# A parallel attention and feed-forward kernel: a unit's first attention product three steps ahead of the rest, and seven small moves of splits, a relu, additions and a norm

## The chip, the cores and the metric

The kernel runs on one core of a Trainium2 chip. The core has five engines that work through their own instruction lists in order and wait for each other through semaphores: PE (TensorE, matmuls; PEld is its weight load), DVE (VectorE), ACT (ScalarE), POOL (GpSimd) and SP (SyncE, which here only issues DMAs; POOL issues some, too). The metric is the device time of one execution in microseconds.

## What is computed

```python
# x (1, 2048, 576); wqkv (576, 1728); wo (576, 576); w1 (576, 4608); w2 (4608, 576), fp32
def attention(xn):                  # 32 heads of 18
    q, k, v = split(xn @ wqkv)
    idx = pos[:, None] - 2 * arange(8)[None, :]     # 8 taps, two rows apart
    logits = where(idx >= 0, einsum("bhsd,bhswd->bhsw", q, k[idx]) * 18 ** -0.5, -1e9)
    return einsum("bhsw,bhswd->bhsd", softmax(logits), v[idx]) @ wo

xn = (x - mean(x)) / sqrt(var(x) + 1e-5)
return x + attention(xn) + relu(xn @ w1) @ w2
```

## The kernel before

**Phases and precision.** The taps are two rows apart, so even and odd rows never meet in the attention. The kernel works in two phases `ph`, the even rows and the odd rows, 1024 rows each in four token blocks `tb` of 256. Every fp32 factor is split into a high part and a remainder (`hi`, `lo`), and a product is three matmuls. `two` (L171) makes such a split: ACT copies the high part (L172), DVE subtracts to get the low part (L176), or POOL does where `pooled` is set (L174). The relu is split in the same manner (`relu_parts`, L765): ACT L769 writes the high part, DVE L773 the low part. `c_parts` calls it for one block of the hidden layer.

**Feed-forward.** The first 6 of a phase's 36 blocks of 128 hidden columns are done in 24 plain slots of one block and one token block each. The other 30 are done in pairs by a Strassen scheme: 30 groups `g` of eight steps (`group`, and `step` inside it). Two groups share one pair of W1 blocks (the even group is the first), and each group does two of the four token blocks. `sw_prep` splits the combined W1 matrices of a pair (A11, A12, A22, S1 to S4 and a remainder "rem"), `sw_mix` forms them on POOL (L924), `w2_split` splits W2. Products collect in PSUM banks called a, q, r and f, which come from the rings `ph` (a, q) and `pm` (r, f) of two buffers each. `seed` (L992, ACT) copies one bank into a new one, `keep` (L996, ACT) puts a bank aside as m5 or u3 (named m and u in the profile), `plus` (L1001, DVE) adds a bank to it. The second layer collects in `po`, and `evict` (L722, ACT; then a POOL DMA at L728 that accumulates in memory) takes it out. `prologue` is group 0 with the last slots woven in; `tail_end`, `last_group`, `seam` and `epilogue` finish a phase. In a step, `rows` issues the matmuls of the first layer, `after` their followers, `fire` the events of a table, and `o_half` the second layer.

**Attention.** The heads are done in four units `u` of 8 heads. Unit 0 is projected in the slots, units 1 to 3 in groups 5, 11 and 17 and the one after each (`QKV_G`), with the weights split by `wq_split`. From two groups later, 7, 13 and 19, the unit's attention is put on a background list `bg` of DVE operations: per tap window i a product (`qk_mul`, L575) and a sum (`qk_sum`, L578), then the softmax, then products and additions with V (L610, L617) and a transposition (L622). The first window, i = 7, reads only the unit's own rows; later ones read rows that `halos` fetches by DMA. `run_bg(margin)` takes operations off this list as long as the planner's clock of DVE does not pass that of PE by more than the margin; a small or negative margin takes fewer. The list's place in the program is thus the order on DVE.

**Output projection.** The attention's result goes through memory (`od`) and comes back transposed. `ot_plan` lists its work: `wo_rest` loads three pieces of WO (DMA, L267; event "wl"), `wo_split` splits each (ACT L172 `wq<-att` 128x576) a given time on the planner's clock after "wl", `ot_in` loads the result, `ot_split` (L683 to L685) splits it. `ot_one` issues at most one item at each place where it is asked, in every step.

**Start.** In the first slots of phase 0 the x rows are loaded in eight blocks, normalised (`stats`, then `norm`: L340 on DVE, or L337 and L338 on ACT with `act`), and transposed on PE (`make_xt`: L359 and L366 on ACT, L362 and L369 on DVE take the parts). `o_out` adds x to the first output blocks on DVE (L888).

## Time and profile before

| | us |
|---|---|
| median of 3 runs | 1127.75 |
| lowest and highest | 1126.84, 1128.8 |
| profiled execution, its own time | 1129.04 |
| span of its profile, first to last instruction | 1127.3 |
| mean granted TensorE clock | 0.998 |
| PE busy | 1108.6 |
| DVE busy | 850.8 |
| ACT busy | 571.0 |
| POOL busy | 367.9 |

A row of a timeline reads: start in us from the start of the span, duration, engine, line of the kernel, operation, result <- inputs with their shapes, a count, and in square brackets how long the engine stood idle before it and on what that ended. Where a tile is named `ar`, it is the arena of split weights and hidden blocks; `st` holds the staged weights, `ev` what is evicted, `att` the attention's arena, `pr` its products, and `xT`, `xS` the transposed rows and their Strassen sums. A tile with two buffers or more has one name for all.

### The profile page before, as it was taken

Reading aid. Unit: us, or ns where it says so; the run is one execution under the profiler, and the core shown is the slowest. Engines: PE = TensorE matmul, PEld = TensorE weight load, DVE = VectorE, ACT = ScalarE, POOL = GpSimd, SP = SyncE. Lnnn points to the kernel's source line nnn. Section 1 sums busy time; section 2 is a strip of 40 time slices with the busy share of each in tenths; the row PEclk is TensorE's granted clock in tenths of the full one; section 3 lists DMA queues with packets and bytes.
Section 4 is the critical chain, followed back from the end, with each engine's and each line's share of the span. In section 5 each row is a group of like instructions: output and inputs, shape, how many; then the busy total and the mean of one; then the engine's idle time right before and its main releaser. Section 6 shows DMA issues by size and latency. Waiting matters only on the chain.

```text
span 1127.3 us, 37950 instructions
## 1 busy us (share of the span) xinstructions
PE 1108.6 (98%) x16410; PEld 1093.4 (97%) x16410; DVE 850.8 (75%) x1249; ACT 571.0 (51%) x1348; POOL 367.9 (33%) x382
## 2 busy tenths in 40 slices
PE   8999999999999999999999999999999999999998
PEld 8999999999999999999999999999999999999998
DVE  7676898798898898984327339978888988989651
ACT  4433563564465356566434346535645644655550
POOL 2314342333333234433322225323413423344321
PEclk9999999999999999999999999999999999999999
DMA  7369895795696497889957258759848956878995
GB/s 235 125 170 221 180 186 90 152 201 105 123 218 128 87 208 144 161 163 267 264 82 156 44 124 169 131 93 216 167 80 175 189 103 152 164 153 154 197 178 135
DMA packets 136598, 177.26 MB, mean 157 GB/s; under 512 B 27872, under 2 KB 83936, under 8 KB 136400
## 3 DMA queue, kind: packets, MB, share of 16 engines
q0 software_dynamic: 37632, 81.40, 46.2%
q1 hardware_dynamic: 98080, 92.55, 28.0%
q8 instruction: 129, 2.11, 0.7%
q10 hardware_dynamic: 720, 0.89, 0.2%
q14 instruction: 37, 0.30, 0.1%
HBM read 74.07 MB, written 96.22 MB: 151 GB/s over the span
## 4 chain that ended last, share of the span: by engine, by line
PE 86%; DVE 6%; issue 3%; ACT 2%; DMA 2%; POOL 0%; DVEq 0%; ACTq 0%; POOLq 0%
PE po L163 28%; PE po L142 21%; PE ph L163 14%; PE pm L163 11%; PE pm L142 5%; PE ph L142 3%; PE ph L130 1%; DVE ar L176 1%; DVE ar L773 1%; PE po L130 1%; DMA out<-ev 1%; DVE pr L575 1%; DVE att L622 1%; ACT ev L722 1%; DVE pr L610 0%
## 5 line engine op out<-in xcount | busy, mean ns | idle before, releaser
L163 PE MATMUL po<-ar 64*128 64x320 f32 (+1 forms) x5760 | 473.9, 290 | 0.4 <-ACT ev L722 0.3
L163 PEld LDWEIGHTS po<-ar 64*128 64x128 f32 x5760 | 415.8, 185 | 2.0 <-ACT ev L722 0.6
L163 PE MATMUL ph<-xT,ar 64*128 64x256 f32 x2520 | 323.3, 276 | 4.8 <-ACT pm L992 2.6
L728 POOL DMA_DIRECT2D out<-ev x128 | 152.9, 1195 | 495.9 <-ACT ev L722 347.4
L163 PEld LDWEIGHTS ph<-xT,ar 64*128 64x128 f32 x2520 | 288.5, 185 | 8.6 <-ACT pm L992 5.2
L163 PE MATMUL pm<-xS,ar 64*128 64x256 f32 x2160 | 261.9, 276 | 3.5 <-ACT u L996 2.8
L163 PEld LDWEIGHTS pm<-xS,ar 64*128 64x128 f32 x2160 | 238.9, 185 | 5.0 <-ACT u L996 3.2
L722 ACT ACTIVATE ev<-po 128x512 f32<-128x512 f32 (+1 forms) x266 | 171.4, 650 | 122.3 <-PE po L163 69.5
L176 DVE TENSOR_TENSOR ar<-st,ar 128x256 fp32r<-128x256 f32 (+3 forms) x232 | 155.6, 675 | 76.0 <-ACT ar L172 70.1
L172 ACT ACTIVATE ar<-st 128x256 fp32r<-128x256 f32 (+3 forms) x304 | 151.3, 503 | 12.1 <-PE po L142 3.5
L142 PE MATMUL po<-wq,xT 64*128 64x432 f32 x1296 | 136.2, 353 | 0.0
L142 PEld LDWEIGHTS po<-wq,xT 64*128 64x128 f32 x1296 | 124.1, 185 | 1.0 <-ACT ev L722 0.2
L174 POOL TENSOR_TENSOR ar<-st,ar 128x256 fp32r<-128x256 f32 (+2 forms) x72 | 80.5, 1122 | 118.0 <-ACT ar L172 117.8
L924 POOL TENSOR_TENSOR st<-st 128x256 f32<-128x256 f32 x120 | 113.1, 948 | 15.2 <-DMA st<-in_w 10.9
L163 PE MATMUL ph<-xS,ar 64*128 64x256 f32 x720 | 102.6, 275 | 1.3 <-ACT ph L992 1.1
L163 PEld LDWEIGHTS ph<-xS,ar 64*128 64x128 f32 x720 | 94.2, 185 | 2.5 <-ACT ph L992 1.8
L575 DVE TENSOR_TENSOR pr<-att 128x1152 f32<-128x1152 f32 x64 | 89.4, 1409 | 0.1
L610 DVE TENSOR_TENSOR pr<-att 128x1152 f32<-128x1152 f32 x64 | 89.1, 1412 | 0.4
L578 DVE TENSOR_REDUCE att<-pr 128x64 f32<-128x1152 f32 x64 | 85.4, 1343 | 0.0
L142 PE MATMUL po<-ar 64*128 64x256 f32 (+1 forms) x984 | 71.4, 290 | 0.0
L617 DVE TENSOR_TENSOR pr<-pr 128x1152 f32<-128x1152 f32 x64 | 68.8, 1075 | 1.4
L773 DVE SCALAR_TENSOR_TENSOR ar<-ph,ar 128x256 fp32r<-128x256 f32 x96 | 39.1, 418 | 39.9 <-ACT ar L769 39.5
(121 smaller groups left out, 1373.2 us busy)
## 6 DMA issues: line engine op xcount, KB each, us to landing
out<-ev POOLq DMA_DIRECT2D x128, 576.0 KB, 7.1
st<-in_w SPq DMA_DIRECT2D x72, 288.0 KB, 5.6
st<-in_w SPq DMA_DIRECT2D x63, 256.0 KB, 3.4
att<-att SPq DMA_DIRECT2D x16, 441.0 KB, 4.4
att<-in_wqkv SPq DMA_DIRECT2D x28, 216.0 KB, 6.6
od<-att SPq DMA_DIRECT2D x32, 160.0 KB, 5.0
att<-in_x SPq DMA_DIRECT2D x14, 288.0 KB, 3.9
st<-in_w SPq DMA_DIRECT2D x60, 64.0 KB, 5.9
```

The source lines that it names most:

```text
L142: ins = nc.tensor.matmul(o, l[z], r[z], start=start, stop=stop)
L163: b.ins = nc.tensor.matmul(b.ap, l[part], r[part], start=start, stop=stop, skip_group_check=skip)
L172: nc.scalar.activation(hi, src, AF.Copy)
L174: nc.gpsimd.tensor_tensor(lo, src, f32(hi), op=ALU.subtract)
L176: nc.vector.tensor_tensor(lo, src, f32(hi), op=ALU.subtract)
L575: nc.vector.tensor_tensor(pr[i], q, window(k, i), op=ALU.mult)
L578: nc.vector.tensor_reduce(lg[:, i], pr.pop(i).rearrange(heads, d=Dh), axis=AX.X, op=ALU.add)
L610: nc.vector.tensor_tensor(pr[i].rearrange(heads, d=Dh), e, window(v, i).rearrange(heads, d=Dh), op=ALU.mult)
L617: nc.vector.tensor_tensor(o, z[:, :, 0:n], z[:, :, n : 2 * n], op=ALU.add)
L722: nc.scalar.activation(acc[:, :, cols], z[:, :, 0 : cols.stop - cols.start], AF.Copy)
L728: ADDED[ph, tb] = nc.gpsimd.dma_start(rows_of(ph, tb), acc, accum_op=ALU.add)
L924: nc.gpsimd.tensor_tensor(stg(o), stg(a), stg(b), op=op)
```

## The change

Eight edits, in the order of the diff:

1. For units 1 to 3, the first product and sum (window 7) are put on the list at step 1 of groups 7, 13 and 19; the rest (`attention_rest`) at step 4. Before, all of it came at step 4, for unit 3 at the end of step 3.
2. The split of S3 and S4 moves from the end of step 1 to the end of step 2 of each even group.
3. The margin of the background list in `prologue` goes from 0.3 to -0.8.
4. WO splits: 13 instead of 9 on the planner's clock after "wl".
5. In a step the eviction of a 256-column piece comes ahead of the table's "T" events.
6. In group 1 the relu of the kept m5 of group 0 comes a step later, behind a seed.
7. At the seam of the phases, W2 blocks 0 and 2 and two of the five QKV pieces of phase 1 have their low parts on DVE instead of POOL; QKV pieces 3 and 4 stand at the front of their slot.
8. At the start the third W2 load goes behind the x loads; x block 5 is normalised on ACT; the second pair of x additions goes ahead of the transposed parts of x block 4.

```diff
         n, big = NI * W * HG, W * UD
+
+        def more():
+            t["dve"] = max(t["dve"], t["pe"] - 1.5)
+            for f in (qk_mul, qk_sum):
+                bg.append((big, f, (NI - 2,)))
...
         t["dve"] = max(t["dve"], t["pe"] - 1.5)
-        for j in (NI - 1, NI - 2):
-            for f in (qk_mul, qk_sum):
-                bg.append((big, f, (j,)))
...
+        for f in (qk_mul, qk_sum):
+            bg.append((big, f, (NI - 1,)))
+        if u:
+            rest[ph, u] = more
+            return
+        more()
+
+    rest = {}
+
+    def attention_rest(ph, u):
+        rest.pop((ph, u))()
@@ plan_strassen
-                on(ph, a, 1, "O", sw_prep, ph, p, "S3", "S4")
+                on(ph, a, 2, "O", sw_prep, ph, p, "S3", "S4")
...
-            on(ph, g + 2, *((4, "T") if u < NU - 1 else (3, "O")), attention, ph, u)
+            on(ph, g + 2, 1, "T", attention, ph, u)
+            on(ph, g + 2, 4, "T", attention_rest, ph, u)
@@ ot_plan
-            z.append((("ws", kt), wo_split, (ph, kt), None, (("wl", 9 + 3.0 * (kt - 2)),)))
+            z.append((("ws", kt), wo_split, (ph, kt), None, (("wl", 13 + 3.0 * (kt - 2)),)))
@@ prologue
         seed(ph, g, "r", "q")
-        run_bg(0.3)
+        run_bg(-0.8)
@@ step
-            fire(ph, g, i, "T")
             if i % 2 == 0:
                 og, piece = (g - 2, 1 + i // 2) if i < 5 else (g - 1, (i - 6) // 2)
                 if og >= 0 and PIECES[piece][1] == 0:
                     o_evict(ph, og, piece)
+            fire(ph, g, i, "T")
@@ group
-            1: [(c_parts, ph, prev, 0, 1, PC[ph, prev, "m5"])],
+            (1 if prev > 0 else 2): [(c_parts, ph, prev, 0, 1, PC[ph, prev, "m5"])],
@@ seam and the slots of phase 1
-                w2_split(1, 0, (0, 1), True)
+                w2_split(1, 0)
...
-            late(b, w2_split, 1, 2, (0, 1), True)
+            late(b, w2_split, 1, 2)
...
-                late(b + 11 + kt // 3, wq_split, ph, 0, kt, kt % 2 == 1)
+                (first if kt > 2 else late)(b + 11 + kt // 3, wq_split, ph, 0, kt)
@@ start
-    w2_load(0, 2)
     for i in range(4, NI):
         load_x(i)
+    w2_load(0, 2)
...
-    s5 = stats(0, 5, parts=True)
+    s5 = stats(0, 5, parts=True, act=True)
...
-    for f in x4[:3]:
+    x4[0]()
+    o_out(2, (1,))
+    norm(0, 5, True)
+    for f in x4[1:]:
         f()
-    norm(0, 5)
-    o_out(2, (1,))
-    x4[3]()
```

On PE both kernels have the same instructions in the same order. New lines shift the numbers below them: L722, L769, L773, L992, L996, L1001 are L736, L783, L787, L1006, L1010, L1015 in the changed kernel.

DVE in phase 0, from the transposition at the end of unit 2's attention (L622) on, which is group 19; before:

```order
L622 STREAM_TRANSPOSE att<-att 128x8x128
L625 STREAM_TRANSPOSE att<-att 128x8x32
L1001 TENSOR_TENSOR m_7378<-m_7378,ph 128x256
L773 SCALAR_TENSOR_TENSOR ar<-u_7474,ar 128x256
L773 SCALAR_TENSOR_TENSOR ar<-m_7378,ar 128x256
L176 TENSOR_TENSOR ar<-st_7015,ar 128x256
L176 TENSOR_TENSOR ar<-st_7015,ar 128x320
L575 TENSOR_TENSOR pr<-att 128x1152
L773 SCALAR_TENSOR_TENSOR ar<-pm,ar 128x256
L176 TENSOR_TENSOR ar<-st,ar 128x256
L578 TENSOR_REDUCE att<-pr 128x64
```

and with the change:

```order
L622 STREAM_TRANSPOSE att<-att 128x8x128
L625 STREAM_TRANSPOSE att<-att 128x8x32
L1015 TENSOR_TENSOR m_7383<-m_7383,ph 128x256
L787 SCALAR_TENSOR_TENSOR ar<-u_7477,ar 128x256
L787 SCALAR_TENSOR_TENSOR ar<-m_7383,ar 128x256
L176 TENSOR_TENSOR ar<-st_7019,ar 128x256
L575 TENSOR_TENSOR pr<-att 128x1152
L176 TENSOR_TENSOR ar<-st_7019,ar 128x320
L787 SCALAR_TENSOR_TENSOR ar<-pm,ar 128x256
L176 TENSOR_TENSOR ar<-st,ar 128x256
L578 TENSOR_REDUCE att<-pr 128x64
```

The product L575 has moved from behind the second half of the W2 split to ahead of it. In groups 7 and 13 it comes to the same place from behind the relu `ar<-pm` and the L176 that follows it.

ACT in phase 1 around the three WO splits (`wq<-att` 128x576), in the last group, before:

```order
L722 ACTIVATE ev<-po 128x2x256
L172 ACTIVATE wq<-att 128x576
L722 ACTIVATE ev<-po 128x2x320
L996 ACTIVATE u_20921<-pm 128x256
L172 ACTIVATE ar<-st_20586 128x320
L172 ACTIVATE wq<-att 128x576
L769 ACTIVATE ar<-u_20921 128x256
L769 ACTIVATE ar<-m_20855 128x256
L172 ACTIVATE ar<-st_20624 128x256
L992 ACTIVATE ph<-ph 128x256
L722 ACTIVATE ev<-po 128x2x256
L172 ACTIVATE wq<-att 128x576
```

and with the change:

```order
L736 ACTIVATE ev<-po 128x2x320
L1010 ACTIVATE u_20922<-pm 128x256
L172 ACTIVATE ar<-st_20589 128x320
L172 ACTIVATE wq<-att 128x576
L783 ACTIVATE ar<-u_20922 128x256
L783 ACTIVATE ar<-m_20858 128x256
L172 ACTIVATE ar<-st_20627 128x256
L1006 ACTIVATE ph<-ph 128x256
L736 ACTIVATE ev<-po 128x2x256
L172 ACTIVATE wq<-att 128x576
L736 ACTIVATE ev<-po 128x2x320
```

The first split now stands where the second one stood, behind the eviction of 320 columns, the `keep` of u and a W2 split; the second where the third stood. The third has gone on to between the relu `ar<-pm` and the seed `pm<-ph`.

DVE in the prologue of phase 0, the relu of the first hidden block (`ar<-ph`) and what stands around it, before:

```order
L575 TENSOR_TENSOR pr<-att 128x1152
L773 SCALAR_TENSOR_TENSOR ar<-ph,ar 128x256
L313 BN_STATS bst<-att 128x6 x2
L316 BN_AGGR mv<-bst 128x2
L317 TENSOR_SCALAR mv<-mv 128x1
L1001 TENSOR_TENSOR u_2132<-u_2132,pm 128x256
L773 SCALAR_TENSOR_TENSOR ar<-u_2132,ar 128x256
L1001 TENSOR_TENSOR m_2014<-m_2014,ph 128x256
L773 SCALAR_TENSOR_TENSOR ar<-m_2014,ar 128x256
```

and with the change:

```order
L787 SCALAR_TENSOR_TENSOR ar<-ph,ar 128x256
L313 BN_STATS bst<-att 128x6 x2
L316 BN_AGGR mv<-bst 128x2
L317 TENSOR_SCALAR mv<-mv 128x1
L1015 TENSOR_TENSOR u_2134<-u_2134,pm 128x256
L787 SCALAR_TENSOR_TENSOR ar<-u_2134,ar 128x256
L1015 TENSOR_TENSOR m_2017<-m_2017,ph 128x256
L575 TENSOR_TENSOR pr<-att 128x1152
L787 SCALAR_TENSOR_TENSOR ar<-m_2017,ar 128x256
```

The product has gone from ahead of the relu to behind the addition to m5.

24 lines of the change are left out of this document (12 added, 12 removed).

## The prediction

> **What bounds the kernel now.** I read the page's busy times first, then the chain of waits, then what TensorE (PE) waited for, and at each large wait the timeline of all engines around it.
>
> ```profile
> PE 1108.6 (98%) x16410; PEld 1093.4 (97%) x16410; DVE 850.8 (75%) x1249; ACT 571.0 (51%) x1348; POOL 367.9 (33%) x382
> ...
> PE 86%; DVE 6%; issue 3%; ACT 2%; DMA 2%; POOL 0%; DVEq 0%; ACTq 0%; POOLq 0%
> ```
>
> PE is busy for 1108.6 of the span's 1127.3 us and holds 86% of the chain. An edit that takes no matmul away can win only out of the 18.7 us in which PE stands, and out of a little more that lies inside a busy row whose matmul starts late. Here the order on PE is the same in both kernels, so the change does nothing but move when PE's operands are ready. The question is which of PE's waits it touches:
>
> ```profile
> engine line waited for: us in total, times, longest us
> PE pm L163 <- ACT u L996: 2.8, 2, 2.3
> PE ph L163 <- ACT pm L992: 2.6, 6, 0.9
> PE ph L163 <- DVE ar L773: 1.8, 3, 0.6
> ...
> PE ph L163 <- ACT ph L992: 1.1, 3, 0.4
> PE po L130 <- DVE ev L888: 0.9, 1, 0.9
> PE pm L142 <- DVE wq L176: 0.8, 1, 0.8
> ```
>
> The rows give the total, the count and the longest of each kind. They are short waits at a few places, each behind one instruction that stands ahead of the needed one on an in-order engine. The edits move such instructions at five of these places, and I cost each there.
>
> **The start (x additions before the norm of x block 5).** PE waits for the second pair of x additions:
>
> ```profile
> 25.09 0.68 DVE L362 TENSOR_TENSOR xT<-pm,xT 128x512 fp32r<-128x512 f32 x1
> 25.69 0.57 DVE L340 TENSOR_SCALAR att<-att,mv,rstd 128x576 f32<-128x576 f32 x1
> 26.18 0.82 DVE L888 TENSOR_TENSOR ev<-po,att 128x256 f32<-128x256 f32 x2
> ...
> 26.74 1.25 PE L130 MATMUL po<-ar 128*128 128x256 f32 x6 [0.93 <-DVE ev L888]
> ...
> 25.85 0.38 ACT L769 ACTIVATE ar<-ph 128x256 fp32r<-128x256 f32 x1 [1.01 <-PE ph L130]
> ...
> 32.48 0.78 ACT L338 ACTIVATE att<-att,rstd 128x576 f32<-128x576 f32 x1
> ```
>
> The pair moves into the place of L362, from 26.18 to 25.09, 1.09 us earlier. The wait is 0.93 and goes whole, if what moves to ACT does no harm: the norm is there two instructions of about 0.78, of which ACT's idle 1.01 before 25.85 takes most; 1.56 - 1.01 = 0.55 is pushed onto the next relu. L362 falls back by 0.82. Bounds: 0.93 - 0.55 = 0.4 to 0.93. I take 0.8, because the relu's second half on DVE stands behind the same L362 and L888 anyway. The later W2 load is one transfer ahead of nothing that PE waits for in these rows: 0.
>
> **The prologues (margin 0.3 to -0.8, relu of m5 after the seed).** In phase 0:
>
> ```profile
> 115.71 1.36 DVE L575 TENSOR_TENSOR pr<-att 128x1152 f32<-128x1152 f32 x1
> 116.98 0.42 DVE L773 SCALAR_TENSOR_TENSOR ar<-ph,ar 128x256 fp32r<-128x256 f32 x1
> 117.45 0.96 PE L163 MATMUL ph<-xT,ar 64*128 64x256 f32 x9 [0.64 <-DVE ar L773]
> ...
> 120.22 0.42 ACT L769 ACTIVATE ar<-m 128x256 fp32r<-128x256 f32 x1 [0.88 <-DVE m L1001]
> 120.54 0.37 ACT L992 ACTIVATE ph<-ph 128x256 f32<-128x256 f32 x1
> ```
>
> The relu L773, whose bank PE wants back, stands behind one attention product of 1.36. The product goes behind the sums L1001, so L773 starts about 1.2 earlier and the 0.64 is gone. What the product holds instead is the low half of the relu of m5 (L773 `ar<-m`), which is read only a step later; that is its cover, and without it 1.36 would come back once. The seed L992 stands behind that relu, which itself waits for L1001: 120.54 against a release at 120.22 or before, so 0.32 at least. Phase 1 has the same order; of the waits for seeds into `ph` (1.1 in 3) and for L773 (1.8 in 3) I give it 0.3. Together 0.64 + 0.32 + 0.3 = 1.3; from 0.6 (the product alone) to 1.8.
>
> **Group 19 of both phases (first attention product three steps ahead).**
>
> ```profile
> 398.96 0.49 DVE L176 TENSOR_TENSOR ar<-st,ar 128x320 fp32r<-128x320 f32 x1 [1.28 <-ACT ar L172]
> 399.37 2.71 DVE L575 TENSOR_TENSOR pr<-att 128x1152 f32<-128x1152 f32 x1
> 402.01 0.41 DVE L773 SCALAR_TENSOR_TENSOR ar<-pm,ar 128x256 fp32r<-128x256 f32 x1
> ...
> 399.65 1.20 POOL L924 TENSOR_TENSOR st<-st 128x256 f32<-128x256 f32 x1
> ...
> 402.51 0.37 ACT L992 ACTIVATE pm<-ph 128x256 f32<-128x256 f32 x1 [3.00 <-DVE ar L773]
> 402.93 0.38 PE L163 MATMUL ph<-xT,ar 64*128 64x256 f32 x1 [0.86 <-ACT pm L992]
> ...
> 953.85 0.37 ACT L992 ACTIVATE pm<-ph 128x256 f32<-128x256 f32 x1 [2.99 <-DVE ar L773]
> ```
>
> For the last unit the product runs right before L773, beside POOL, and takes 2.71 instead of the 1.36 above. L773 is late, the seed L992 with it, and PE waits 0.86; in phase 1 the seed shows the same 2.99. Now the product stands before the W2 split of 398.96, where DVE is idle for 1.28: it would begin at 398.96 - 1.28 = 397.68 and end at 399.04 (at 1.36), the split at 399.5, L773 at 399.9 instead of 402.4. PE could have gone on at 402.93 - 0.86 = 402.07, so about 1.7 us of room is left and both waits go: 2 x 0.86 = 1.7. Even a product of 2.71 at the new place ends at 400.4, L773 at 401.3, still in time. Units 1 and 2 (groups 7 and 13) had their product behind L773 and no such wait; theirs changes nothing. Bounds: 0 (the seed finds another holder) to 2.0, both waits with the late starts around them.
>
> The Trainium skill (SBUF — State Buffer, Who interferes with whom) says that a VectorE instruction with two SBUF inputs and a GpSimd one that reads SBUF exclude each other, and that whoever is second is blocked until the first is done. The 2.71 agrees: 399.65 + 1.20 is the end of L924, and 1.36 after it is 402.2, against a recorded end of 402.08. By that rule the early product, being first, is not stretched, and the sum stays as it is.
>
> **The seam (W2 and QKV splits from POOL to DVE).**
>
> ```profile
> 609.15 1.59 POOL L174 TENSOR_TENSOR wq<-att,wq 128x432 fp32r<-128x432 f32 x1
> ...
> 609.48 1.74 DVE L176 TENSOR_TENSOR wq<-att,wq 128x432 fp32r<-128x432 f32 x1 [0.30 <-ACT wq L172]
> ...
> 614.62 0.59 DVE L176 TENSOR_TENSOR wq<-att,wq 128x432 fp32r<-128x432 f32 x1
> 615.27 0.46 PE L142 MATMUL pm<-wq,xT 64*128 64x432 f32 x2 [0.81 <-DVE wq L176]
> ```
>
> PE waits 0.81 for the last QKV half. The split costs 0.59 alone and 1.74 beside POOL's. With all five on DVE, two more of 0.59 come (+1.2), the stretch of 1.74 - 0.59 = 1.15 goes, and the last two stand ahead of two W1 halves and three block subtractions instead of behind the W1 halves. The last half then ends some 0.8 earlier. The two W2 splits add about 4 x 0.5 on DVE, each like the 0.49 for 320 columns above. The work of DVE in the stretch in which POOL did them, by windows (length, then busy time of PE, PEld, DVE, ACT, POOL):
>
> ```profile
> 530.00:560.00 30.00, 29.73 (x452) 28.63 (x451) 11.61 (x24) 17.36 (x39) 11.34 (x11) 1.00 1.07 257
> ```
>
> DVE is busy for 11.61 of 30, so I cost them at nothing; if that cover fails they cost 2.0 once. I take 0.7; from -1.2 to 0.9.
>
> **The end of phase 1 (WO splits one place later on ACT).**
>
> ```profile
> 1067.61 0.68 ACT L172 ACTIVATE wq<-att 128x576 fp32r<-128x576 f32 x1 [4.34 <-DMA att<-wo]
> 1068.20 0.69 ACT L722 ACTIVATE ev<-po 128x640 f32<-128x640 f32 x1
> 1068.78 0.38 ACT L996 ACTIVATE u<-pm 128x256 f32<-128x256 f32 x1
> 1069.21 0.58 PE L163 MATMUL pm<-xS,ar 64*128 64x256 f32 x1 [2.34 <-ACT u L996]
> ...
> 1072.27 0.42 ACT L769 ACTIVATE ar<-m 128x256 fp32r<-128x256 f32 x1 [1.88 <-DVE m L1001]
> ...
> 1076.26 0.37 ACT L992 ACTIVATE pm<-ph 128x256 f32<-128x256 f32 x1 [0.68 <-DVE ar L773]
> ```
>
> This is the longest single wait: ACT stands 4.34 us for a WO load, and an eviction and L996, which frees PE's bank, are queued behind it. In the new order both precede the split, and PE's 2.34 goes. The split still waits for its load, until about 1067.6, and now holds the relu of u, then the relu of m and the seed of `ph`. In before, ACT idles 1.88 ahead of the relu of m, so there is room for most of it; PE, being 2.34 earlier, can use up that room. The third split now stands before the seed of `pm`, which had 0.68 of idle, as long as the split. I take 2.3. The other wait for L996 (2.8 - 2.3 = 0.5) comes from an eviction that waits for the DMA of the one before; that DMA starts earlier now: 0.3. Together 2.6; from 0.3 (the wait reappears at the seed) to 3.0.
>
> **Nothing else.** In the 28 even groups the W1 split S3/S4 goes from ahead of a seed to behind it, and the W2 split behind an eviction. PE does not wait for those seeds (L992 into `ph`: 1.1 in 3 of 60), so no gain; the loss is a rival below.
>
> Sum: 0.8 + 1.3 + 1.7 + 0.7 + 2.6 = 7.1. I take off 0.8, a ninth, since each removed wait can uncover a shorter one behind it: 6.3. The profiled run took 1129.04 (span 1127.3 and 1.7 around it), 1.3 over the median of 1127.75. Against its own time the sum gives 1122.7; from the median 1121.4, and I say 1121.5.
>
> **Rivals.**
> A. The WO load still decides. The split at its new place holds ACT until the load lands, and PE, earlier by 2.34, meets the wait at the relu of u or the seed. For: the load's time is set by the sync queue, not by ACT. Against: the 1.88 of idle. The 2.6 shrinks to 0.3: 1127.75 - 4.0 = 1123.8.
>
> B. Moved to DVE and ACT, the work costs what it frees, at the start and the seam: 0.8 - 0.55 there, and -1.2 for two extra halves here. The sum is 1.3 + 1.7 + 2.6 + 0.25 - 1.2 = 4.6, less its ninth 4.1: 1123.6. With A as well 1125.9, which is no measurable change.
>
> C. Slower: the two W1 splits of an even group now stand next to each other, right before the relu L773 into `pm` and the seed behind it.
>
> ```profile
> 1060.39 0.37 ACT L992 ACTIVATE pm<-ph 128x256 f32<-128x256 f32 x1 [1.06 <-PE ph L163]
> ```
>
> ```profile
> L176 DVE TENSOR_TENSOR ar<-st,ar 128x512 fp32r<-128x512 f32 x92 | 64.5, 701 | 34.4 <-ACT ar L172 30.8 <-PE po L142 1.0
> ```
>
> If DVE has no room there, each of the 28 groups loses one such half, 0.70: 28 x 0.70 = 19.6 against the 6.3, so 1141.1. It decides from the point at which the seed is more than its room late: 1.06 in group 28 before ACT's own wait ends, and 1.7 more in group 19's arithmetic. Against it: the attention work that precedes the splits on DVE is only exchanged with them, so the sum ahead of L773 is the same; it is late only where DVE idles for the split's ACT half. A partial case, 0.3 in each of 28, is 8.4 - 6.3 = +2.1, 1129.9.
>
> D. The change is not felt, because each wait reappears one instruction later: 1127.75.
>
> **Chances.** The forecast 0.68; A 0.10; B 0.07; A with B or D 0.08; C, whole or partial, 0.07. A change of 0.2% is 2.3 us, about what a measurement of this kernel can tell from none: faster means below 1125.5. The forecast, A and B lie there, 0.85; A with B and D give 0.08 for the same; C gives 0.07. The range holds the forecast's own sum with all upper bounds (0.93 + 1.8 + 2.0 + 0.9 + 3.0 = 8.6, 1119.1, and a little for the spread of the runs, 1118.5) and reaches up to A with B at 1125.9. With the lower bounds alone (0.4 + 0.6 + 0 - 1.2 + 0.3 = 0.1) nothing would be won; that all five fall there is D.
>
> **What would show it.** Right: in the list of PE's waits the rows for L888, for the QKV half, for L996 above 1 us, and for the seeds into `pm` above 0.5 are gone, and PE's busy time stays within 1 us while the span falls by 6. The product L575 of group 19 lasts 1.4 and ends before the split of 320 columns. The WO split on ACT still shows a wait for its load, but with L996 ahead of it. Wrong: a PE wait for `ph` seeds of over 1 us near the WO split (A); PE waits at the seam's QKV matmuls or for x block 5's transposes (B); a wait for `pm` seeds in many even groups (C); a forecast off in size, with all of these absent, would mean that waits inside busy rows were counted wrongly.

## The result and the profile after

The changed kernel takes 1121.52 us (median of 6 runs, 1119.13 to 1122.37), the kernel before 1127.95 (6 runs, 1126.84 to 1129.12). The ratio is 0.9939 with a 95% interval of 0.9926 to 0.9952: faster by 6.4 us. The profiled execution of the change took 1121.96, with a span of 1119.9.

The busy times of the changed kernel, from the page:

```profile
PE 1105.7 (99%) x16410; PEld 1089.5 (97%) x16410; DVE 844.5 (75%) x1254; ACT 573.1 (51%) x1350; POOL 358.8 (32%) x377
```

The instructions of PE are as many as before, and its busy time fell by 2.9. A busy row of PE holds late starts of matmuls inside it, so 2.9 of the gain came out of rows that counted as busy. About 1.6 of that is a stretch of the profile before in which the granted clock was half (see wo9).

What PE waited for in the changed kernel (total, times, longest):

```profile
PE po L163 <- ACT ar L783: 1.7, 1, 1.7
...
PE ph L163 <- ACT pm L1006: 1.3, 4, 0.5
PE ph L163 <- ACT ph L1006: 1.1, 3, 0.4
PE po L130 <- ACT ar L172: 1.0, 1, 1.0
PE ph L163 <- DVE ar L787: 0.8, 2, 0.5
```

The rows for the x additions, the QKV half and the keep of u are gone, and the seeds into `pm` have no wait above 0.5. Two rows are new: a relu (1.7, now the longest) and a W2 split at the start (1.0). Both matter below.

Since PE runs the same 16410 instructions in the same order, the n-th of one profile can be set against the n-th of another, and the difference of their start times can be followed through the program. The table gives its change in us in stretches of the kernel before (times of its profile), negative where PE gained on the kernel before. The names are those of the experiments.

| | 16-22 | 22-33 | 110-127 | 395-408 | 525-560 | 600-620 | 940-960 | 1060-1070 | 1070-1084 | 1084-1090 | 1090-1126 | rest | all |
|---|---|---|---|---|---|---|---|---|---|---|---|---|---|
| the change | 1.7 | -1.2 | -1.2 | -1.4 | -0.3 | -1.2 | -1.3 | -3.0 | -1.4 | 1.6 | 0.0 | 0.5 | -7.1 |
| start_w2 | -0.1 | -1.2 | -1.1 | -1.4 | -0.2 | -1.3 | -1.4 | -3.0 | -1.8 | 1.2 | 0.0 | 1.4 | -8.9 |
| end_pr | 0.8 | -1.1 | -1.2 | -1.4 | -0.5 | -1.3 | -1.3 | -3.0 | -1.6 | 0.0 | 0.0 | 0.7 | -9.9 |
| wo9 | -0.1 | -1.2 | -1.2 | -1.3 | -0.5 | -1.3 | -1.3 | -1.3 | 0.2 | 0.0 | 0.0 | -0.3 | -8.3 |
| attn_old | 1.3 | -1.1 | -1.2 | -0.1 | 0.0 | -1.3 | 0.0 | -3.0 | -1.0 | 2.9 | 0.0 | -0.1 | -3.6 |
| seam_old | 0.2 | -1.1 | -1.1 | -1.2 | -0.4 | 0.0 | -1.3 | -3.0 | -1.8 | 1.0 | 0.0 | -0.4 | -9.0 |
| prol_old | 0.2 | -1.2 | -0.1 | -1.4 | -0.3 | -1.2 | -1.4 | -3.0 | -1.0 | 3.0 | 0.1 | -0.5 | -6.7 |
| s34_old | 0.6 | -1.2 | -1.2 | -1.4 | -0.1 | -1.3 | -1.3 | -3.0 | -1.1 | 1.3 | 0.0 | 1.8 | -6.9 |
| more_prod | 0.1 | -1.1 | -1.2 | -0.2 | 1.2 | -1.3 | 1.0 | -3.0 | -0.5 | 0.0 | 0.0 | 0.3 | -4.7 |
| best | 0.3 | -1.1 | -1.1 | -1.2 | -0.4 | -1.3 | -1.4 | -3.0 | -0.6 | 0.0 | 0.0 | 0.7 | -9.1 |
| best_dve | 0.1 | -0.8 | -1.2 | -1.3 | -0.3 | -1.3 | -1.3 | -3.0 | -1.9 | 0.0 | 0.0 | -0.2 | -11.4 |
| only_wo13 | 0.4 | -0.1 | 0.0 | 0.0 | 0.5 | 0.0 | 0.0 | -3.0 | -1.2 | 0.1 | 0.0 | -0.4 | -3.6 |
| wo_15 | 0.4 | -0.8 | -1.1 | -1.4 | 4.4 | -1.2 | -1.3 | -3.0 | -1.2 | 0.0 | 3.5 | 1.3 | -0.4 |

Most columns repeat to 0.1 or 0.2 wherever the order in them is the same. Five do not: 16-22, 525-560, 1070-1084, 1084-1090 and "rest". In those PE waits, through ACT, for a DMA (in 525-560 of more_prod for an eviction that stood 1.76 for its buffer), or the granted clock is half for some us (see wo9), and a profile shows one execution of it. The columns 1060-1070 and 1070-1084 also hold such a stretch of the kernel before, 1.6 in sum. That is why a part that is undone is read from its own column here, and the medians only say whether the sum goes the same way.

Medians of the experiments, each with the median of the kernel before run beside it, and their ratio:

| | median us | kernel before | ratio | 95% interval |
|---|---|---|---|---|
| start_w2 | 1119.60 | 1128.60 | 0.9920 | 0.9907 to 0.9933 |
| end_pr | 1119.32 | 1128.60 | 0.9921 | 0.9905 to 0.9938 |
| wo9 | 1123.83 | 1128.60 | 0.9953 | 0.9938 to 0.9969 |
| attn_old | 1124.50 | 1128.60 | 0.9960 | 0.9946 to 0.9974 |
| seam_old | 1122.46 | 1128.83 | 0.9943 | 0.9930 to 0.9957 |
| prol_old | 1122.08 | 1128.83 | 0.9939 | 0.9926 to 0.9951 |
| s34_old | 1121.36 | 1128.83 | 0.9932 | 0.9919 to 0.9946 |
| more_prod | 1124.59 | 1128.83 | 0.9964 | 0.9950 to 0.9979 |
| best | 1119.63 | 1128.31 | 0.9919 | 0.9906 to 0.9933 |
| best_dve | 1118.37 | 1128.31 | 0.9914 | 0.9900 to 0.9927 |
| only_wo13 | 1126.55 | 1128.31 | 0.9986 | 0.9977 to 0.9995 |
| wo_15 | 1129.85 | 1128.94 | 1.0010 | 1.0001 to 1.0019 |

The kernel before has medians from 1127.95 to 1128.94 in these sets. A kernel is therefore compared with the change by its gain on the kernel before beside it, which is 6.4 for the change. By the intervals, gains that differ by less than about 2 are not told apart.

### The profile page after: what moved, and what is told of

It reads as the page before. It is cut to its first block, busy times and chain, and to the rows that moved or that the text cites. A ratio compares the mean times of both kernels' runs of the same rounds, so it can differ in the third digit from the quotient of the medians.

```text
span 1119.9 us, 37923 instructions
## 1 busy us (share of the span) xinstructions
PE 1105.7 (99%) x16410; PEld 1089.5 (97%) x16410; DVE 844.5 (75%) x1254; ACT 573.1 (51%) x1350; POOL 358.8 (32%) x377
## 4 chain that ended last, share of the span: by engine, by line
PE 87%; DVE 4%; issue 4%; DMA 2%; ACT 2%; POOL 1%; DVEq 0%; ACTq 0%; POOLq 0%
PE po L163 28%; PE po L142 22%; PE ph L163 14%; PE pm L163 11%; PE pm L142 5%; PE ph L142 4%; DMA out<-ev 2%; PE ph L130 1%; DVE ar L176 1%; PE po L130 1%; DVE ar L787 1%; DVE att L622 1%; PE po L119 0%; DMA st<-in_w 0%; ACT ev L736 0%
## 5 line engine op out<-in xcount | busy, mean ns | idle before, releaser
L163 PE MATMUL po<-ar 64*128 64x320 f32 (+1 forms) x5760 | 456.8, 289 | 1.8 <-ACT ar L783 1.7
L163 PEld LDWEIGHTS po<-ar 64*128 64x128 f32 x5760 | 398.7, 184 | 3.3 <-ACT ar L783 1.9
L163 PE MATMUL ph<-xT,ar 64*128 64x256 f32 x2520 | 319.8, 275 | 2.6 <-ACT pm L1006 1.3
L163 PE MATMUL pm<-xS,ar 64*128 64x256 f32 x2160 | 258.8, 275 | 0.6
L163 PEld LDWEIGHTS pm<-xS,ar 64*128 64x128 f32 x2160 | 236.1, 184 | 1.9 <-ACT u L1010 0.6
L736 ACT ACTIVATE ev<-po 128x512 f32<-128x512 f32 (+1 forms) x266 | 171.5, 651 | 128.1 <-PE po L163 65.6
L176 DVE TENSOR_TENSOR ar<-st,ar 128x256 fp32r<-128x256 f32 (+3 forms) x236 | 156.4, 675 | 73.7 <-ACT ar L172 73.2
L142 PE MATMUL po<-wq,xT 64*128 64x432 f32 x1296 | 133.8, 353 | 0.3 <-ACT ev L736 0.3
L142 PEld LDWEIGHTS po<-wq,xT 64*128 64x128 f32 x1296 | 119.9, 184 | 3.2 <-ACT ev L736 0.6
L174 POOL TENSOR_TENSOR ar<-st,ar 128x256 fp32r<-128x256 f32 (+1 forms) x68 | 75.7, 1116 | 126.3 <-ACT ar L172 126.3
L610 DVE TENSOR_TENSOR pr<-att 128x1152 f32<-128x1152 f32 x64 | 87.1, 1378 | 0.6
L575 DVE TENSOR_TENSOR pr<-att 128x1152 f32<-128x1152 f32 x64 | 87.2, 1367 | 0.2
L787 DVE SCALAR_TENSOR_TENSOR ar<-ph,ar 128x256 fp32r<-128x256 f32 x96 | 39.0, 418 | 40.6 <-ACT ar L783 40.2
```

What stands on the lines that cost most here:

```text
L142: ins = nc.tensor.matmul(o, l[z], r[z], start=start, stop=stop)
L163: b.ins = nc.tensor.matmul(b.ap, l[part], r[part], start=start, stop=stop, skip_group_check=skip)
L174: nc.gpsimd.tensor_tensor(lo, src, f32(hi), op=ALU.subtract)
L176: nc.vector.tensor_tensor(lo, src, f32(hi), op=ALU.subtract)
L575: nc.vector.tensor_tensor(pr[i], q, window(k, i), op=ALU.mult)
L610: nc.vector.tensor_tensor(pr[i].rearrange(heads, d=Dh), e, window(v, i).rearrange(heads, d=Dh), op=ALU.mult)
```

## The experiments

**attn_old: the early product alone undone.**

```diff
-        if u:
-            rest[ph, u] = more
-            return
         more()
...
-            on(ph, g + 2, 1, "T", attention, ph, u)
-            on(ph, g + 2, 4, "T", attention_rest, ph, u)
+            on(ph, g + 2, *((4, "T") if u < NU - 1 else (3, "O")), attention, ph, u)
```

> The changed kernel with the attention list as before (all of a unit's products at step 4 of its group, for the last unit at the end of step 3). Theory 1: the product L575 stands again right before the relu in group 19 of both phases and takes 2.7, and PE waits about 0.85 there in each; with the late starts around it +1.7 to +2.6, about 1123.5. Rival: the gain in group 19 came from the other edits or the order of the two W1 splits, and nothing returns: 1121.5.

DVE's timeline in group 19 of phase 0, in the changed kernel:

```profile
397.27 1.35 DVE L575 TENSOR_TENSOR pr<-att 128x1152 f32<-128x1152 f32 x1
398.63 0.49 DVE L176 TENSOR_TENSOR ar<-st,ar 128x320 fp32r<-128x320 f32 x1
399.04 0.42 DVE L787 SCALAR_TENSOR_TENSOR ar<-pm,ar 128x256 fp32r<-128x256 f32 x1
```

and with the list undone (L784 is the relu there):

```profile
398.10 0.49 DVE L176 TENSOR_TENSOR ar<-st,ar 128x320 fp32r<-128x320 f32 x1 [1.28 <-ACT ar L172]
398.51 2.71 DVE L575 TENSOR_TENSOR pr<-att 128x1152 f32<-128x1152 f32 x1
401.15 0.41 DVE L784 SCALAR_TENSOR_TENSOR ar<-pm,ar 128x256 fp32r<-128x256 f32 x1
```

The early product fills the 1.28 in which DVE waited, takes 1.35 and not 2.71, and the relu follows 1.77 after the product's start instead of 2.64. Undone, both columns of group 19 go from -1.4 and -1.3 to about 0, and the median gain falls from 6.4 to 4.1. Theory 1 holds. The columns hold 1.3 to 1.4 each, more than the 0.86 that the list of waits shows, since PE also ran slower than its pace around the wait: in phase 0 of the kernel before, the matmul behind the wait started 1.16 after the one ahead of it, against 0.14 in the changed kernel, and two later ones started 0.22 after the ones ahead of them instead of 0.11.

**more_prod: how much room the new place has.** The first product of the last unit is issued twice in phase 0 and three times in phase 1:

```diff
-            nc.vector.tensor_tensor(pr[i], q, window(k, i), op=ALU.mult)
+            for _ in range(1 + (1 + ph if u == NU - 1 and i == NI - 1 else 0)):
+                nc.vector.tensor_tensor(pr[i], q, window(k, i), op=ALU.mult)
```

> The changed kernel, and the first product of the last unit (group 19) is issued twice in phase 0 and three times in phase 1, to the same place with the same values. It stands at its new place ahead of the W2 split. The prediction says that there is room: the relu behind it ends at 399.46 in the changed kernel's profile, and PE came to wait in the kernel before only when it ended later than about 401.6, which is some 2.0 later (less what PE gained, 0.6). Theory 1: one extra product (1.35) costs nothing in phase 0; two (2.70) make PE wait 0.5 to 1.3 in phase 1. Rival: POOL's work there stretches the extra products to 2.7 each, and both phases wait 1 us or more. Second rival: no room at all, each extra product costs its 1.35: +4.

DVE and POOL in group 19 of both phases (the added line shifts all numbers behind it by one):

```profile
395.61 3.33 DVE L576 TENSOR_TENSOR pr<-att 128x1152 f32<-128x1152 f32 x2
398.86 1.02 DVE L176 TENSOR_TENSOR ar<-st,ar 128x320 fp32r<-128x320 f32 x1
399.81 0.41 DVE L788 SCALAR_TENSOR_TENSOR ar<-pm,ar 128x256 fp32r<-128x256 f32 x1
...
946.79 5.13 DVE L576 TENSOR_TENSOR pr<-att 128x1152 f32<-128x1152 f32 x3
...
948.84 1.86 POOL L939 TENSOR_TENSOR st<-st 128x256 f32<-128x256 f32 x1
```

One extra product was not free: PE lost 1.4 - 0.2 = 1.2 of group 19's gain in phase 0, and 1.3 + 1.0 = 2.3 in phase 1. The extra work is not 1.35 a piece, because the products and the W2 split behind them run into POOL: the relu came 4.20 after the first product's start in phase 0 and 5.46 in phase 1 (952.25, by the same view), against 1.77 in the changed kernel, so 2.4 and 3.7 late. Take away what PE lost, and both phases say the same: the new place has 1.2 to 1.4 us of room, not the 1.7 of the prediction. Its remark that even a product of 2.71 would be in time holds only just, at 1.36 more, or not at all.

**seam_old: the W2 and QKV splits back on POOL.**

```diff
-                w2_split(1, 0)
+                w2_split(1, 0, (0, 1), True)
...
-            late(b, w2_split, 1, 2)
+            late(b, w2_split, 1, 2, (0, 1), True)
...
-                (first if kt > 2 else late)(b + 11 + kt // 3, wq_split, ph, 0, kt)
+                late(b + 11 + kt // 3, wq_split, ph, 0, kt, kt % 2 == 1)
```

> The changed kernel with the seam as before: W2 blocks 0 and 2 and two QKV pieces have their low parts on POOL again, and pieces 3 and 4 come at the end of their slot. Theory 1 (term 0.7 of the prediction, 1.1 to 1.5 in the two profiles): PE waits about 0.8 again for the low part of the last QKV piece, whose neighbours on DVE are stretched by POOL; +0.7 to +1.5. Rival: the two extra pieces and the W2 halves on DVE cost as much elsewhere, so that undoing them changes nothing or gains up to 1.

DVE's low parts of the QKV pieces in the changed kernel, three and then two:

```profile
606.87 1.65 DVE L176 TENSOR_TENSOR wq<-att,wq 128x432 fp32r<-128x432 f32 x3 [0.98 <-ACT wq L172]
...
610.37 1.12 DVE L176 TENSOR_TENSOR wq<-att,wq 128x432 fp32r<-128x432 f32 x2
```

and DVE, POOL and PE with the seam undone:

```profile
605.76 1.74 DVE L176 TENSOR_TENSOR wq<-att,wq 128x432 fp32r<-128x432 f32 x1 [0.30 <-ACT wq L172]
...
605.44 1.59 POOL L174 TENSOR_TENSOR wq<-att,wq 128x432 fp32r<-128x432 f32 x1
...
611.55 0.46 PE L142 MATMUL pm<-wq,xT 64*128 64x432 f32 x2 [0.81 <-DVE wq L176]
```

Three pieces on DVE alone take less (1.65) than one beside POOL's (1.74). The wait of 0.81 is back to the hundredth, and the column 600-620 goes from -1.2 to 0.0. The medians do not show it: the gain on the kernel before is 6.4 with the seam undone, too. The two further W2 splits on DVE cost nothing: the column 525-560 stays within 0.2. Theory 1 holds by the column.

The Trainium skill (SBUF — State Buffer, Who interferes with whom) says that a VectorE instruction with two SBUF inputs and a GpSimd one that reads SBUF exclude each other. The rows agree: POOL's piece ends at 605.44 + 1.59 = 607.03, and 0.55 of work (1.65 / 3) after that is 607.58, against a recorded end of 607.50.

**prol_old: the prologue's margin back at 0.3.**

```diff
-        run_bg(-0.8)
+        run_bg(0.3)
```

> The changed kernel with the margin in the prologues back at 0.3, the relu of m5 staying behind the seed. Theory 1: in phase 0 the attention product (1.36) stands again ahead of the relu, and PE's wait of 0.64 near 117 returns, with the late start +0.6 to +0.9; phase 1 at most +0.1. Rival: the relu moved behind the seed is what won there, and nothing returns.

The changed kernel, DVE and ACT in the prologue of phase 0:

```profile
116.03 0.41 DVE L787 SCALAR_TENSOR_TENSOR ar<-ph,ar 128x256 fp32r<-128x256 f32 x1
...
119.18 1.35 DVE L575 TENSOR_TENSOR pr<-att 128x1152 f32<-128x1152 f32 x1
...
119.36 0.37 ACT L1006 ACTIVATE ph<-ph 128x256 f32<-128x256 f32 x1 [0.88 <-DVE m L1015]
```

and PE with the margin undone:

```profile
116.34 0.96 PE L163 MATMUL ph<-xT,ar 64*128 64x256 f32 x9 [0.65 <-DVE ar L787]
```

The wait of the kernel before (0.64) is back, and the column goes from -1.2 to -0.1. Phase 1 hardly moves. The column also says that the relu of m5 behind the seed is worth nothing by itself: it stayed in this kernel, and the column lost 1.1 of 1.2. The medians do not show it (a gain of 6.8 against 6.4 for the change).

**s34_old: the two moves that were costed at nothing.**

```diff
-                on(ph, a, 2, "O", sw_prep, ph, p, "S3", "S4")
+                on(ph, a, 1, "O", sw_prep, ph, p, "S3", "S4")
...
+            fire(ph, g, i, "T")
             if i % 2 == 0:
...
-            fire(ph, g, i, "T")
```

> The changed kernel with two parts undone: the split of S3 and S4 is again at the end of step 1 of each even group, and the 256-column eviction again behind the table's T events. Theory 1 (costed at nothing): no matmul moves by more than 0.3 us in any even group, total within 0.5. Rival C of the prediction: the splits standing together cost up to 0.7 per even group, so that undoing them gains up to 19. Another rival: they win 0.1 to 0.2 in many groups, and undoing costs 2 to 5.

PE's busy time in the groups, by windows (length, then PE, PEld, DVE, ACT, POOL), for the changed kernel:

```profile
676.00:1060.00 384.00, 382.62 (x5842) 378.92 (x5840) 334.75 (x443) 208.65 (x507) 135.20 (x138) 1.00 0.77 152
```

and with the two parts undone:

```profile
676.00:1060.00 384.00, 382.31 (x5826) 378.21 (x5826) 335.90 (x443) 207.89 (x505) 133.67 (x138) 1.00 0.78 152
```

In the same 384 us PE is busy for 382.3 or 382.6: neither 28 losses of 0.7 nor a gain. The "rest" of 1.8 is made of three losses of about 0.6 behind evictions, near 126, 517 and 865, of a kind that the other profiles have at other places (the change itself 0.6 near 351, end_pr 1.0 near 957). The median, 1121.36, is that of the change (1121.52). The prediction's slower rival is out.

**wo9: the WO splits back at 9.**

```diff
-            z.append((("ws", kt), wo_split, (ph, kt), None, (("wl", 13 + 3.0 * (kt - 2)),)))
+            z.append((("ws", kt), wo_split, (ph, kt), None, (("wl", 9 + 3.0 * (kt - 2)),)))
```

> The changed kernel with the WO splits back at 9 instead of 13 on the planner's clock. Theory 1 (the prediction's term of 2.6): ACT stands again several us for the WO load ahead of the keep of u, PE waits about 2.3 there, and the wait of 1.67 for the eviction's DMA a little later shrinks or goes, since that DMA has the time meanwhile; the sum is +1 to +2.8 us, near 1123.5. Rival: the 1.67 stays as well, +2.3 to +4, near 1125. Second rival: the other edits already brought the load early enough, 1121.5.

ACT in the last group of phase 1, changed kernel:

```profile
1060.48 0.38 ACT L1010 ACTIVATE u<-pm 128x256 f32<-128x256 f32 x1
...
1062.90 0.69 ACT L172 ACTIVATE wq<-att 128x576 fp32r<-128x576 f32 x1 [1.68 <-DMA att<-wo]
...
1078.22 0.60 ACT L736 ACTIVATE ev<-po 128x512 f32<-128x512 f32 x1 [4.24 <-DMA out<-ev]
1078.71 0.41 ACT L783 ACTIVATE ar<-m 128x256 fp32r<-128x256 f32 x1
...
1079.18 1.08 PE L163 MATMUL po<-ar 64*128 64x256 f32 x10 [1.67 <-ACT ar L783]
```

and with the splits undone:

```profile
1059.49 0.68 ACT L172 ACTIVATE wq<-att 128x576 fp32r<-128x576 f32 x1 [3.44 <-DMA att<-wo]
1060.09 0.69 ACT L736 ACTIVATE ev<-po 128x640 f32<-128x640 f32 x1
1060.67 0.38 ACT L1010 ACTIVATE u<-pm 128x256 f32<-128x256 f32 x1
```

In the changed kernel the keep of u is done before the split starts to wait; undone, it stands behind that wait again. From 1060 to 1084 the change gained 4.4 and the undone kernel 1.1.

Not all of the 4.4 is the wait itself. Behind the wait of 2.34 the profile of the kernel before shows half the clock for 3.4 us, and the changed kernel the full clock throughout (windows as above; behind POOL's busy time stand the granted TensorE clock, the DMA share and GB/s):

```profile
1069.00:1072.40 3.40, 3.19 (x26) 3.19 (x28) 2.78 (x5) 1.52 (x5) 2.10 (x2) 0.50 1.06 306
```

```profile
1060.00:1086.00 26.00, 24.18 (x363) 23.05 (x363) 13.21 (x28) 16.29 (x34) 6.93 (x6) 1.00 1.00 233
```

In the stretch at half clock matmuls of 256 columns start 0.21 apart, otherwise 0.11. PE works for some 3.2 us of it, so it costs 1.6; the wait's end gave 2.5. The profile of wo9 has no such stretch, which is why it gained 1.1 although PE waited 1.43 for the keep of u, 0.60 for the seed of `ph` and 0.52 for the next keep. It is the fastest of that kernel's six executions (1120.76, median 1123.83); four of the others list a mean clock of 0.998, which is what one such stretch leaves.

But some 15 us behind the first split of the changed kernel an eviction stands for 4.24 on ACT, because its buffer, one of two, is still being written out, and the relus behind it hold PE for 1.67. The undone kernel has no such wait (column 0.0), since it is late already. Where that DMA stands on POOL, in the changed kernel and then in the kernel before, with the eviction that needs its buffer there:

```profile
1067.72 1.20 POOL L742 DMA_DIRECT2D out<-ev  x1 [4.80 <-ACT ev L736]
```

```profile
1075.25 1.20 POOL L728 DMA_DIRECT2D out<-ev  x1 [3.97 <-ACT ev L722]
...
1084.18 0.60 ACT L722 ACTIVATE ev<-po 128x512 f32<-128x512 f32 x1 [1.38 <-PE pm L163]
```

With the change the buffer was held for 10.5, from 1067.72 to 1078.22; before, for at most 8.9, and the eviction waited for PE instead. So the edit is worth 3.3 - 1.6 = 1.7 net in these profiles, and 1.7 in the medians (gains of 6.4 and 4.8). Theory 1 holds, though PE's wait at the keep was 1.43 in this profile and not 2.3.

**only_wo13: this edit alone in the kernel before** (9 to 13 in the same line).

> The kernel before with one part of the change alone: the WO splits at 13 instead of 9. Theory 1: at the WO split PE gains the 2.97 between 1060 and 1070 us that the changed kernel shows there, and some more behind it, and gives back 1 to 3 at the eviction's DMA near 1086: 0.5 to 2.8 in sum, about 1126.5. Rival: alone it gains all of 3 to 4 us, near 1124.5, and the eviction's wait belongs to another edit. Second rival: without the other edits the load comes no earlier than PE needs it, and nothing is gained.

The profiled execution gains 3.0 and 1.2 in the same columns and gives nothing back, but it is the fastest of 11: 1125.56, with a median of 1126.55 and the slowest at 1128.70. The median gain, 1.8, is less than half of the profile's 4.2. But 1.6 of the 4.2 is the half clock in the profile of the kernel before, and 12 of the 15 executions of that kernel run beside this one list a mean clock of 0.999 or 1.0, too high for such a stretch. Without it 2.6 is left, which is the upper end of the median's interval (0.6 to 2.6). A give-back in other executions, as theory 1 has it, is possible but not shown; only this one has a trace.

**end_pr: a third place for an eviction.** The buffer of the attention's products is free by then.

```diff
+        if ph:
+            hold["last"] = prp.tile([P, 2, 2, D], F32, name="pr")
+            EV[ph, 2 * ((g - 1) % 2), "o"] = hold["last"][:, 1], []
         run_bg(1.0)
...
-        z = prp.tile([P, 2, 2, D], F32, name="pr")
-        for j in range(2):
+        z = hold["last"] if ph else prp.tile([P, 2, 2, D], F32, name="pr")
+        for j in (1,) if ph else range(2):
             EV[ph, 2 * (g % 2) + j, "o"] = z[:, 1 - j], []
```

> The changed kernel, and in phase 1 the last-but-one eviction of the groups goes to a free part of the attention's product buffer instead of the ring of two eviction buffers. In the changed kernel that eviction waits 4.24 us for the DMA of an earlier one, until 1078.22, with two relus behind it on ACT, and PE waits 1.67. Theory 1: the wait came out because the WO wait ahead of it went and the DMA is the next thing late; with a third place for the result the 1.67 goes, about 1120. Rival: the relus or the next eviction wait for something else, and less than 0.5 is gained.

The eviction and the relu behind it:

```profile
1073.70 0.60 ACT L736 ACTIVATE pr<-po 128x512 f32<-128x512 f32 x1 [0.84 <-PE po L163]
1074.42 0.42 ACT L783 ACTIVATE ar<-m 128x256 fp32r<-128x256 f32 x1
```

The eviction waits for PE now and no longer for a DMA. The column 1084-1090 is 0.0 here and in the three later kernels that have this edit; without it, with the WO splits at 13 and all else of the change in place or one other part undone, it was between 1.0 and 3.0 in six profiles (the late `more_prod` had 0.0). In the two of about 3.0, attn_old and prol_old, some 1.2 of it is a stretch at half clock behind the wait. The median is 1119.32, a gain of 9.3 against 6.4 for the change. Theory 1 holds, and the give-back has its cause.

**start_w2: the third W2 load back ahead of the x loads.**

```diff
+    w2_load(0, 2)
     for i in range(4, NI):
         load_x(i)
-    w2_load(0, 2)
```

> The changed kernel with one part undone: the third W2 load goes again ahead of the loads of x blocks 4 to 7. In the changed kernel PE waits 1.03 us at 19.51 for the ACT split of that W2 block, which waits for its DMA until 19.04 (17.46 in the kernel before). Theory 1: the load is late because its transfer shares the DMA engines with the x loads issued ahead of it; with the order undone the split starts near 17.5, the wait of 1.03 is gone, and the kernel gains some 1.0 to 1.7 us on the changed one (about 1120.0). Rival: the late landing is chance of one execution; then the wait is in neither profile or in both, and the time stays near 1121.5.

In the changed kernel the split of that block, on ACT, and PE behind it:

```profile
19.04 0.77 ACT L172 ACTIVATE ar<-st 128x256 fp32r<-128x256 f32 x2 [3.56 <-DMA st<-in_w]
...
19.51 2.35 PE L130 MATMUL po<-ar 128*128 128x256 f32 x12 [1.03 <-ACT ar L172]
```

and the same split in the kernel before:

```profile
17.46 0.78 ACT L172 ACTIVATE ar<-st 128x256 fp32r<-128x256 f32 x2 [1.81 <-DMA st<-in_w]
```

It starts 1.6 later with the change. With the load back in its place the column 16-22 is -0.1 and the additions keep their -1.2. But the late landing is not in every execution: the eight profiles with the load behind the x loads have 1.7, 0.8, -0.1, 1.3, 0.2, 0.2, 0.6 and 0.1 in this column, mean 0.6; the five with it ahead -0.1, 0.3, 0.1, 0.4 and 0.4, mean 0.2. The median gain is 9.0 against 6.4 for the change, a difference that is more than this column can give. The place of the load is worth some 0.4 on average by the profiles. Part of the rest may be the clock: three of the change's six executions list a mean clock of 0.998, and one of the six here.

**best: both remedies.** The edits of start_w2 and end_pr together.

> The changed kernel with both remedies: the third W2 load ahead of the x loads again, and the eviction at the end of phase 1 in the product buffer. Theory 1: the two late waits are of different places, so they add: PE's 1.03 near 19 and 1.67 near 1079 are both gone in every execution, some 2.5 us below the changed kernel, about 1118.5, and the executions scatter less than 1119.1 to 1122.4. Rival: the late W2 load was rare, so that this is as fast as the second remedy alone, 1119.3.

The sum did not appear: 1119.63, a gain of 8.7, against 9.0 and 9.3 for either alone. The waits of its profile show what came instead:

```profile
PE ph L163 <- ACT ph L1006: 2.2, 4, 1.0
```

```profile
1062.69 0.69 ACT L172 ACTIVATE wq<-att 128x576 fp32r<-128x576 f32 x1 [2.61 <-DMA att<-wo]
```

The WO load landed later relative to ACT, the split waited 2.61 for it instead of 1.68, and the seed of `ph` behind it held PE for 1.0. That is the prediction's rival A, at 1.0 instead of its 2.3. Other profiles have it, too, and they fix its size: where the split waited 1.89, 2.04, 2.25, 2.54 and 2.61 (s34_old, attn_old, prol_old, more_prod, best), PE waited 0.29, 0.44, 0.65, 0.94 and 1.01 for the seed, each time 1.60 less; where it waited 1.68 or less, the list shows no such wait. The new place covers 1.60 us of the load's wait. The rival of the expectation, that the second remedy carries the gain, fits.

**best_dve: x block 5 normalised on DVE,** at the same place.

```diff
-    s5 = stats(0, 5, parts=True, act=True)
+    s5 = stats(0, 5, parts=True)
...
-    norm(0, 5, True)
+    norm(0, 5)
```

> The same, but x block 5 is normalised on DVE, at the place that the norm has on ACT in the changed kernel (behind all four x additions). Theory 1: what wins at the start is the place of the additions alone; between 22 and 33 us PE gains about 1.17 on the kernel before, as with the norm on ACT. Rival: the norm of 0.58 on DVE holds up the low part of the transposed block 4 and the relu behind it, PE waits for them, and up to 0.6 of the 1.17 is lost.

The column 22-33 gains 0.8 instead of 1.1 or 1.2: the norm on ACT is worth about 0.3, and the place of the additions the rest. Yet it is the fastest version of all: 1118.37 (1117.43 to 1119.56, 5 runs), ratio 0.9914 with an interval of 0.9900 to 0.9927. Its lead on `best` is within the scatter of both and has no cause in the edit.

**wo_15: the splits another step later,** 13 to 15 in best_dve.

> The kernel with both remedies and x block 5 normalised on DVE, and the WO splits at 15 instead of 13, which puts the first of them behind the seed of `ph`, between two evictions. In the kernel with both remedies the first split waited 2.61 us for its load, until 1062.69, and the seed behind it was late (PE waits for such a seed up to 1.0). Theory 1 (rival A of the prediction holds in some executions): with the seed ahead of the split, PE's wait for it is at most 0.4, and between 1060 and 1076 us PE gains about 4.1 on the kernel before in every execution; about 1118.0, or as fast as the one before within 0.5, with less scatter. Rival: the split's wait now holds the eviction of 320 columns, and PE waits for the output bank or the next keep instead, +0.5 to +2.

At the place meant it did what theory 1 said: 3.0 + 1.2 = 4.2 gained from 1060 to 1084 (1.6 of it the half clock of the kernel before). But it was slower than the kernel before, and neither theory had the reason. PE at the seam and at the very end:

```profile
538.86 0.74 PE L142 MATMUL po<-wq,att 64*128 64x256 f32 x8 [2.08 <-ACT att L697]
...
1113.81 0.41 PE L142 MATMUL po<-wq,xS 64*128 64x320 f32 x1 [2.08 <-ACT xS L697]
```

The WO splits are in one list with the splits of the attention's result (L697), and the planner issues at most one item of it at a place. With the WO splits two units later, the last of the result's splits found no place and was issued only when the matmul needed it: 4.4 at the seam, 3.5 at the end. Of the 4.4 some 1.7 is a stretch at half clock behind the wait. The number stands for both phases, and the seam had no wait to lose. The profiled execution, 1128.42, is the fastest of the 11; the other ten list mean clocks of 0.994 to 0.997, which would be two to four such stretches each.

## Why the prediction was right, step by step

The sum of 6.3 and the time of 1121.5 were right, and the sign of every one of the five places too (of the start on average: the profiled execution lost 1.7 - 1.2 = 0.5 there), but the terms are right to different degrees, and errors of both signs met. That 6.3 and the measured 6.4 agree to 0.1 is in part luck.

- **The start, 0.8.** Here a step failed: "The later W2 load is one transfer ahead of nothing that PE waits for in these rows: 0." The additions gained 1.2, more than the 0.8. The load cost 1.7 in the profiled execution and some 0.4 on average; the row to read was the split that stood until 17.46 for its DMA, with PE close behind it. The 0.55 that the norm on ACT was to push on did not show; on DVE the norm costs 0.3 more.
- **The prologues, 1.3.** Measured 1.2 in phase 0 and 0.2 in phase 1 (664 to 676 us). The relu behind the seed, credited with 0.32 + 0.3, gave at most 0.1 in phase 0; the margin gave 1.1, since the wait of 0.64 was not all that the late relu cost.
- **Group 19, 1.7.** The mechanism was shown both ways, by undoing it and by adding to it. The size was 1.4 + 1.3 = 2.7, since it was taken from the gap of 0.86 alone. The room was 1.2 to 1.4, not 1.7.
- **The seam, 0.7.** 1.2 to 1.3, and the cover for the W2 splits was there.
- **The end, 2.6.** The size came out at 3.0 + 1.4 - 1.6 = 2.8, but not for the reasons given. The wait before the keep of u and what followed it were worth 4.4, of which 2.5 is the wait and 1.6 the half clock behind it in the profile of the kernel before. The prediction left that stretch out, although the mean clock of 0.998 pointed to it, and most executions of the kernel before that list a clock do not have it to lose. The idle 1.88 that it counted on as cover for the load came out as 1.60. The term "that DMA starts earlier now: 0.3" had the wrong sign one eviction later: that DMA started 7.5 earlier and PE was 8 earlier, the DMA held its buffer longer, and the wait grew. Undoing the edit gave back 1.7 of the 2.8; the other 1.1 was there without it, in a profile with no stretch at half clock.
- **Nothing else.** Shown by s34_old: nothing.
- **The ninth taken off,** 0.8 for waits uncovered behind those removed, was of the right kind and too small: 1.7 + 1.6 came up in the profiled execution, and what made up for it were the terms that were too low.

Of the rivals, A (the load still decides) came up in five profiles of experiments, at 0.3 to 1.0 and never at its 2.3; B was wrong at the seam and at the start, where the loss came from a load and not from the norm; C was excluded; D was not seen. The sign given for a wrong step, PE's busy time within 1 us, was itself wrong: it fell by 2.9, because late starts behind a wait and matmuls at half clock (1.6 of it) lie inside busy rows.

## What to carry to other kernels

Where an engine is busy for 98% and the order on it stays, cost each edit by the one instruction that stands ahead of the needed one in its queue, and take the loss from the pace of the busy engine around the wait, not from the gap alone: in the prologue, group 19 and the seam it was 1.5 to 1.7 times the gap. Read the granted clock by windows around the longest waits as well: here one of 2.34 had 1.6 more behind it at half clock, in the execution that was profiled. After every wait that goes, ask which buffer's DMA was hidden by it: a ring of two was enough at the old speed and short by 1.6 at the new one, and a third place, borrowed from a buffer that was free, got it back. A number that sets a planner's due time moves everything that shares its list, in every phase: 9, 13 and 15 gave 1123.8, 1121.5 and (in best_dve) a step from 1118.4 to 1129.9.

## What the runs showed of the hardware that was not expected

The scatter of this kernel, 3 us between executions of the same program, is not spread over it. The profiles agree to 0.1 or 0.2 us over most stretches that have the same order, and differ by up to 1.8 in the few where an instruction waits for a DMA: the W2 load at the start, the evictions' buffers, the WO load.

The granted clock adds to this. In four of the 14 profiles it is half for 3.41 us in the middle of the program: from 1069.00 in the kernel before, 1081.53 in attn_old, 1078.96 in prol_old and 540.16 in wo_15. In the 3.41 us ahead of each, PE had stood for 1.6 to 2.6. But PE's wait of 1.67 in the changed kernel and the one of 2.08 at 1113.81 in wo_15 passed without such a stretch, so the length of a wait alone does not decide; what does is not shown. One stretch takes 0.0015 off the mean clock of a span. The nine executions of the kernel before beside seam_old fall apart by it: 1127.15 to 1127.88 in the four at 1.0, and 1128.83 to 1129.91 in the five at 0.998. In the other sets the two groups overlap. Only one execution of each kernel has a trace, so that the DMA waits and these stretches make up the scatter of the medians is inferred.

Beside a POOL operation DVE's product is not slowed evenly but stands. With three products in a row (5.13 us for three of 1.35) the second would end at 946.79 + 2 x 1.35 = 949.49; POOL's addition, 1.20 alone, begun at 948.84, ends at 950.70, which is 949.49 + 1.21; and the third product, 1.35 after 950.70, would end at 952.05, against a recorded 951.92. The two took turns, each whole.
